# Attention tiles of 64 queries for two heads at once, with a block-diagonal q, in place of tiles of 128 queries of one head

## The chip, the cores and the metric

The kernel runs on one core of a Trainium2 chip. Times are device microseconds from runs on the chip; the lower, the better. The engines are TensorE (PE; PEld is its loading of weights), VectorE (DVE), ScalarE (ACT), GpSimd (POOL) and SyncE (SP), whose queue issues the transfers here.

## The reference

Block-causal attention over 8 batches, 8 heads, 576 positions and a head dimension of 64, followed by a feed-forward layer with a rational activation. A query sees all keys of its own block of 64 and of the blocks before it.

```python
scores = scale * np.matmul(q, k.transpose(0, 1, 3, 2))          # (8, 8, 576, 576), scale = 1/8
mask = (pos[:, None] // 64) >= (pos[None, :] // 64)
scores = np.where(mask, scores, -1000000000.0)
attn = np.exp(scores - np.max(scores, axis=-1, keepdims=True))
attn = attn / (np.sum(attn, axis=-1, keepdims=True) + 1e-09)
x = np.matmul(attn, v)                                          # heads side by side: (4608, 512)
h = x @ w_in                                                    # w_in (512, 2048)
g = (a0 + a1*h + a2*h**2 + a3*h**3) / (1 + |b0|*|h| + |b1|*h**2 + 1e-6)
out = g @ w_out                                                 # w_out (2048, 512)
```

## The kernel before

All values are kept as a high and a low part, both float32r (names that end in h and l), and a product of two such values is made of three matmuls: high by high, high by low, low by high.

Attention walks over 32 pairs of heads (8 batches, 4 pairs each). For a pair, `load` fetches q, k and v, `prep` turns q and k with PE and splits them into `hl`, and six transfers on SP's queue copy the parts into `kq`, one for each head: in it the 64 rows of the head hold qh, kh and kl, and the other 64 rows ql, kh and kl, so that a contraction over 128 rows makes two products in one matmul. `scores` then makes, for each of five tiles of queries (64, 128, 128, 128, 128) and each head, two matmuls (L432, L433) into a bank of PSUM. Widths under 256 are padded to 256. A tile of 128 queries spans two blocks, and a 64-column matmul with `mrow` and `mcol` (L436) puts -2^30 on the last 64 keys for its first 64 queries. DVE takes the negated maximum (L437), `expo` runs the exponential on ACT with its sum (L449), POOL multiplies by the reciprocal of the sum `rc` (L458, L462), and `transp` turns P by PE (L481); ACT copies the turned blocks as the high part and DVE subtracts for the low part (L486, L487) into `pt0`, `pt1`, `pt2`. `pv` multiplies by v (L500). There `vpad` holds v's parts with zeros beside them, so that two heads fall on two halves of the output rows:

```python
for i, (vv, pp) in enumerate(((vh, lo), (vh, hi), (vl, hi))):
    nc.tensor.matmul(o[:, s0:w], lhsT=vblock(vv, x), rhs=pp, ...)
```

over 5 key blocks of 320 or 256 columns and 9 of 256. The result is split again (L503 on ACT, L504 on DVE) and stored to `xscr` in DRAM.

A step is one tile of one head; there are ten to a pair. `attn_steps` gives each part its step: expo one step behind the scores, the transposes 9 behind, pv one more, the load of the next pair at step 0, its prep at 3 and 5. Into these steps two other works are dealt by tables: the splitting of the feed-forward weights into two parts (`split_weights`, most of it in the first 60 steps, the rest up to about step 230), and units of the first half of the feed-forward layer (`Ffn`), which begin when the first batch of x is stored. Feed-forward units are `first` (L207, 256 columns), an activation on ACT, DVE and POOL, and `second` (L257, 512 columns). After the attention the second half of the feed-forward layer follows, with 512 columns in both. The written order is then reordered within each engine by a scheduler that estimates times, so the order on the engines is not quite the written one.

Of the kernel before, what the change touches and what calls it, by code (L numbers as in the profile page):

```python
# [9 lines left out]
F32 = mybir.dt.float32  # L10
F32R = mybir.dt.float32r
# [11 lines left out]
CT = 256  # L23
# [10 lines left out]
OFFS = {5:(0,3,5)}  # L34
G1 = 0
# [26 lines left out]
def attn_ffn_kernel(  # L62
# [241 lines left out]
    NQ = [64, 128, 128, 128, 128]  # L304
    Q0 = [0, 64, 192, 320, 448]
    NK = [64, 192, 320, 448, 576]

    wpool = ctx.enter_context(tc.tile_pool(name="wA", bufs=1))
    with ExitStack() as actx:
# [4 lines left out]

        pt0 = [apers.tile([128, 1, 320], F32R, name=f"pt0{x}") for x in "hl"]
        pt1 = [apers.tile([128, 4, 256], F32R, name=f"pt1{x}") for x in "hl"]
        pt2 = [apers.tile([128, 9, 256], F32R, name=f"pt2{x}") for x in "hl"]

        vpad = [apers.tile([128, 128 + 4 * 192], F32R, name=f"vp{x}") for x in "hl"]
        for x in pt1:  # L320
            nc.vector.memset(x[:, 2:4, 0:128].bitcast(F32), 0.0)
        for x in pt2:
            nc.vector.memset(x[:, 7:9, 0:128].bitcast(F32), 0.0)
        for x in vpad:
            nc.vector.memset(x.bitcast(F32), 0.0)


        NP = B * NPAIR
        if G1:
            visits = ([(p, (0, 1, 2)) for p in range(NPAIR - 1)] + [(NPAIR - 1, (0, 1, 2, 3, 4))]  # L330
                      + [(p, (3, 4)) for p in range(NPAIR - 1)]
                      + [(p, (0, 1, 2, 3, 4)) for p in range(NPAIR, NP)])
        else:
            visits = [(p, (0, 1, 2, 3, 4)) for p in range(NP)]
        NV = len(visits)
        st_ = {}

        def load(p):
            b, hp = divmod(visits[p][0], NPAIR)
            h0 = 2 * hp  # L340

            qr, kr = ((ffn.tile([LP, NL, 2, D], F32, name=f"{n}r{p}", tag="x", bufs=XB) if p < RL else
                       att.tile([LP, NL, 2, D], F32, name=f"{n}r{p}", tag="raw", bufs=1)) for n in "qk")
            vr = att.tile([128, 9, D], F32, name=f"vr{p}", tag="vr", bufs=1)
            for j in range(2):
                nc.sync.dma_start(out=qr[:, :, j, :], in_=q[b, h0 + j].rearrange("(c p) d -> p c d", p=LP))
            for j in range(2):
                nc.sync.dma_start(out=kr[:, :, j, :], in_=k[b, h0 + j].rearrange("(c p) d -> p c d", p=LP))
            for j in range(2):
                nc.sync.dma_start(out=vr[j * 64:(j + 1) * 64, 0, :], in_=v[b, h0 + j, 0:64, :])  # L350
                nc.sync.dma_start(out=vr[:, 1 + j::2, :],
                                  in_=v[b, h0 + j, 64:S, :].rearrange("(c p) d -> p c d", p=128))
            st_[p] = dict(qr=qr, kr=kr, vr=vr)

        def prep(p, which):

            s = st_[p]
            if which == 0:
                s["hl"] = att.tile([128, 4, S], F32R, name=f"hl{p}", tag="hl", bufs=1)
            raw, sc = (s["qr"], s["kr"])[which], (QSCALE, 1.0)[which]  # L360
            hl = s["hl"]
            h, l = (hl[:, 0], hl[:, 3]) if which == 0 else (hl[:, 1], hl[:, 2])
            for half in range(2):
                ps = bank(p - 1, f"tp{p}_{which}_{half}")[:, :3 * LP].rearrange("p (c t) -> p c t", c=3)
                for c in range(3):
                    nc.tensor.transpose(ps[:, c, :], raw[:, half * 3 + c].rearrange("p j d -> p (j d)"),  # L366
                                        ident[:LP, :LP])
                cs = slice(half * 288, half * 288 + 288)
                pf = ps.rearrange("p c t -> p (c t)")
                nc.scalar.activation(out=h[:, cs], in_=pf, func=AF.Copy, scale=sc)  # L370
                nc.vector.scalar_tensor_tensor(out=l[:, cs], in0=pf, scalar=sc, in1=h[:, cs].bitcast(F32),
                                               op0=ALU.mult, op1=ALU.subtract)
            if which == 1:


                for j in range(2):
                    kq = att.tile([128, 3, S], F32R, name=f"kq{p}_{j}", tag="kq", bufs=KQB)
                    src = hl[64 * j:64 * j + 64].bitcast(F32)
                    other = kq[64 - 64 * j:128 - 64 * j].bitcast(F32)
                    nc.sync.dma_start(out=kq[64 * j:64 * j + 64].bitcast(F32), in_=src[:, 0:3])  # L380
                    nc.sync.dma_start(out=other[:, 1:3], in_=src[:, 1:3])
                    nc.sync.dma_start(out=other[:, 0], in_=src[:, 3])
                    s["kq", j] = kq

        def vprep(p):
            vr = st_[p]["vr"]
            at = [lambda x: x[0:64, 0:64].unsqueeze(1), lambda x: x[64:128, 64:128].unsqueeze(1),
                  lambda x: x[:, 128:].rearrange("p (b c) -> p b c", c=192)[:, :, 0:64],
                  lambda x: x[:, 128:].rearrange("p (b c) -> p b c", c=192)[:, :, 128:192]]
            of = [vr[0:64, 0:1], vr[64:128, 0:1], vr[:, 1:9:2], vr[:, 2:9:2]]  # L390
            for f, src in zip(at, of):
                vh, vl = (f(x) for x in vpad)
# [3 lines left out]
        def vblock(x, b):  # L396
            c = 0 if b == 0 else 128 + 192 * ((b - 1) // 2) + 64 * ((b - 1) % 2)
            return x[:, c:c + 128]
# [12 lines left out]
        def pieces(t):  # L411
            return [(0, NK[t])] if t < 4 else [(0, 288), (288, 288)]

        def scores(p, t, j):
            s = st_[p]
            nq = NQ[t]
            if j == 0:
                pt = att.tile([128, 2, NK[t]], F32, name=f"p{p}_{t}", tag=f"p{t}", bufs=1)

                pk = att.tile([128, 2, 64], F32, name=f"pk{p}_{t}", tag="pk", bufs=2) if t > 0 else pt  # L420
                nm = att.tile([128, 2, 2], F32, name=f"nm{p}_{t}", tag="nm", bufs=4)
                sm = att.tile([128, 2, 2], F32, name=f"sm{p}_{t}", tag="sm", bufs=4)
                s[t] = (pt, pk, nm, sm)
            pt, pk, nm, sm = s[t]
            kq = s["kq", j]
            qs = slice(Q0[t], Q0[t] + 128)
            banks = []
            for i, (c0, w) in enumerate(pieces(t)):
                ww = max(w, 256)
                ps = ps_a.tile([128, 512], F32, name=f"s{p}_{t}_{j}_{i}", tag="a")  # L430
                last = t > 0 and c0 + w == NK[t]
                nc.tensor.matmul(ps[:, :ww], lhsT=kq[:, 0, qs], rhs=kq[:, 1, c0:c0 + ww], start=True, stop=False)  # L432
                nc.tensor.matmul(ps[:, :ww], lhsT=kq[:, 0, qs], rhs=kq[:, 2, c0:c0 + ww],  # L433
                                 start=False, stop=not last)
                if last:
                    nc.tensor.matmul(ps[:, w - 64:w], lhsT=mrow, rhs=mcol, start=False, stop=True)  # L436
                nc.vector.reduce_max(out=nm[:nq, j, i:i + 1], in_=ps[:nq, :w], axis=AX.X, negate=True)  # L437
                banks.append(ps)
            if t == 4:
                nc.vector.tensor_tensor(out=nm[:, j, 0:1], in0=nm[:, j, 0:1], in1=nm[:, j, 1:2], op=ALU.min)  # L440
            s[t, j] = banks

        def expo(p, t, j):
            s = st_[p]
            nq, n = NQ[t], NK[t]
            pt, pk, nm, sm = s[t]
            banks = s.pop((t, j))
            for i, (c0, w) in enumerate(pieces(t)):
                nc.scalar.activation(out=pt[:nq, j, c0:c0 + w], in_=banks[i][:nq, :w], func=AF.Exp,  # L449
                                     bias=nm[:nq, j, 0:1], scale=1.0, accum_out=sm[:nq, j, i:i + 1])  # L450
# [3 lines left out]
            if t == 4:  # L454
                nc.gpsimd.tensor_tensor(out=sm[:, :, 0], in0=sm[:, :, 0], in1=sm[:, :, 1], op=ALU.add)
# [176 lines left out]
```

## Time and profile before

| | |
|---|---|
| median of 3 runs | 1382.59 us (1381.54 to 1383.46) |
| span of the profiled execution | 1379.1 us; the page gives no other time of its own for it |
| first and last P times V matmul starting a pair | 41.3 and 968.6 us |
| attention's last matmul | starts at 979.5 us |
| mean granted TensorE clock | 0.974 of full speed, 0.86 in the first 100 us and 0.88 in the second |
| moved by DMA | 200.84 MB, 53.6% of 16 engines' span |

The profile's stretches give, for each, how long every engine was busy, the share of the clock that TensorE was granted, the share of time that the 16 DMA engines were busy, and GB/s. In a group of instructions stand the line, the engine, the operation, what it writes and reads, the shapes and how often; then the time in which the group was busy, the mean duration of one in ns, and the idle time before it with what ended it. A timeline row is start, duration, engine, line. Matmuls overlap, so the distance of two starts says what one costs, not its duration.

### The profile page before, as it was taken

To read this page: it belongs to the slowest core of one execution; us is meant where nothing else is said; L and a number is where in the kernel's file an instruction comes from. 1 tells how busy PE (TensorE), PEld (TensorE's weight loads), DVE (VectorE), ACT (ScalarE), POOL (GpSimd) and SP (SyncE) were. 2 spreads that over 40 slices of the span, in tenths; PEclk is the share of its full clock that TensorE was granted. 3 is DMA by queue.
4 is the path that set the end of the run, shared out by engine and by line. 5 is a ranking of instruction groups with operands and counts; after the bars stand their busy time and mean duration, and the time that the engine had idled before them with its cause. 6 is when DMAs were issued, how large, how long until landed. Compare 5 with 4: busy or idle time off the path is not lost.

```text
span 1379.1 us, 24416 instructions
## 1 busy us (share of the span) xinstructions
PE 1278.1 (93%) x8088; PEld 1149.6 (83%) x8088; DVE 1027.2 (74%) x2048; ACT 909.4 (66%) x2250; POOL 958.2 (69%) x1240
## 2 busy tenths in 40 slices
PE   4677899999899979999999999999989999999997
PEld 3667788999888879888998999998979888888885
DVE  5898877787778857887767777776676767676675
ACT  4766767777677756777767777776645655555553
POOL 4889987687678747777767676666556666666654
PEclk9788999999999999999999999999999999999999
DMA  9778556666556655665654555652632233333332
GB/s 216 198 196 238 146 150 166 168 166 181 148 145 150 164 151 132 165 166 153 157 140 123 154 134 122 160 127 65 213 141 77 77 123 123 122 123 123 122 113 86
DMA packets 216925, 200.84 MB, mean 146 GB/s; under 512 B 129504, under 2 KB 184800, under 8 KB 216800
## 3 DMA queue, kind: packets, MB, share of 16 engines
q1 hardware_dynamic: 216736, 199.28, 53.6%
q8 instruction: 65, 1.06, 0.3%
q14 instruction: 60, 0.49, 0.1%
q0 software_dynamic: 64, 0.00, 0.0%
HBM read 98.57 MB, written 44.04 MB: 103 GB/s over the span
## 4 chain that ended last, share of the span: by engine, by line
PE 69%; DVE 9%; POOL 9%; DMA 5%; ACT 3%; issue 3%; SPq 1%; POOLq 0%; DVEq 0%; ACTq 0%
PE h L207 25%; PE o L257 24%; PE o L500 8%; PE t L481 4%; PE s L432 3%; PE s L433 2%; PE tp L366 2%; POOL gl L240 1%; POOL p L462 1%; DMA x<-xscr 1%; POOL u L217 1%; DVE v L231 1%; DVE nm L437 1%; POOL v L216 1%; DMA xscr<-x 1%
## 5 line engine op out<-in xcount | busy, mean ns | idle before, releaser
L207 PE MATMUL h<-x,wih 128*128 128x256 f32 (+1 forms) x1872 | 415.7, 313 | 9.0 <-DMA x<-xscr 7.9
L207 PEld LDWEIGHTS h<-x,wih 128*128 128x128 f32 x1872 | 309.7, 191 | 29.1 <-issue 6.6
L207 PE MATMUL h<-x,wil 128*128 128x256 f32 (+1 forms) x936 | 290.7, 311 | 0.0
L240 POOL TENSOR_TENSOR gl<-s,gh 128x512 fp32r<-128x512 f32 x144 | 188.8, 1313 | 106.4 <-ACT gh L239 103.0
L257 PE MATMUL o<-woh,gl 128*128 128x512 f32 x576 | 232.2, 403 | 12.1 <-POOL gl L240 10.6
L257 PE MATMUL o<-wol,gh 128*128 128x512 f32 x576 | 227.7, 396 | 0.0
L257 PE MATMUL o<-woh,gh 128*128 128x512 f32 x576 | 227.7, 395 | 0.0
L437 DVE TENSOR_REDUCE nm<-s 128x1 f32<-128x288 f32 (+4 forms) x384 | 161.7, 427 | 78.4 <-PE s L436 45.2
L449 ACT ACTIVATE p<-s,nm 128x288 f32<-128x288 f32 (+4 forms) x384 | 184.9, 485 | 48.3 <-DVE nm L437 35.0
L217 POOL TENSOR_TENSOR u<-v,u 128x512 f32<-128x512 f32 x144 | 189.6, 1317 | 9.8
L216 POOL TENSOR_SCALAR v<-u,bab 128x512 f32<-128x512 f32 x144 | 118.9, 826 | 98.1 <-ACT u L214 94.6
L207 PEld LDWEIGHTS h<-x,wil 128*128 128x128 f32 x936 | 178.7, 191 | 8.7
L462 POOL TENSOR_SCALAR p<-p,rc 128x128 f32<-128x128 f32 (+3 forms) x256 | 164.8, 655 | 29.6 <-DVE rc L457 27.7
L218 DVE TENSOR_TENSOR s<-s,h 128x512 f32<-128x512 f32 x144 | 98.5, 684 | 100.1 <-ACT s L215 99.4
L432 PE MATMUL s<-kq 128*128 128x256 f32 (+3 forms) x384 | 137.3, 360 | 24.3 <-DMA kq<-hl 8.9
L224 ACT ACTIVATE v<-u,qcb 128x512 f32<-128x512 f32 x144 | 104.6, 726 | 69.6 <-POOL u L217 68.9
L214 ACT ACTIVATE u<-h 128x512 f32<-128x512 f32 x144 | 85.9, 596 | 94.2 <-PE h L207 90.1
L239 ACT CAST gh<-s 128x512 fp32r<-128x512 f32 x144 | 89.2, 623 | 82.1 <-DVE s L232 81.5
L257 PEld LDWEIGHTS o<-woh,gl 128*128 128x128 f32 x576 | 109.2, 190 | 35.5 <-POOL gl L240 14.3
L257 PEld LDWEIGHTS o<-wol,gh 128*128 128x128 f32 x576 | 109.1, 189 | 22.2
L257 PEld LDWEIGHTS o<-woh,gh 128*128 128x128 f32 x576 | 109.3, 190 | 18.9
L433 PE MATMUL s<-kq 128*128 128x256 f32 (+3 forms) x384 | 120.1, 315 | 0.0
(105 smaller groups left out, 3043.5 us busy)
## 6 DMA issues: line engine op xcount, KB each, us to landing
kq<-hl SPq DMA_DIRECT2D x64, 432.0 KB, 4.3
kq<-hl SPq DMA_DIRECT2D x64, 288.0 KB, 5.3
x<-xscr SPq DMA_DIRECT2D x56, 256.0 KB, 4.2
xscr<-x SPq DMA_DIRECT2D x32, 320.0 KB, 4.7
qr<-in_q_dram SPq DMA_DIRECT2D x64, 144.0 KB, 2.9
kr<-in_k_dram SPq DMA_DIRECT2D x64, 144.0 KB, 3.0
kq<-hl SPq DMA_DIRECT2D x64, 144.0 KB, 4.8
pscr<-os SPq DMA_DIRECT2D x18, 512.0 KB, 2.9
```

Source lines behind the costliest of these rows:

```text
L207: nc.tensor.matmul(h[:, j, :], lhsT=w[:, dc, fs], rhs=xs[dc][:, hl, :], start=(dc == 0 and i == 0), stop=(dc == 3 and i == 2))
L216: nc.gpsimd.tensor_scalar(out=vt, in0=ut, scalar1=b1, scalar2=b0, op0=ALU.mult, op1=ALU.add)
L217: nc.gpsimd.tensor_tensor(out=ut, in0=vt, in1=ut, op=ALU.mult)
L224: nc.scalar.activation(out=vt, in_=ut, func=AF.Ln, bias=qcb)
L240: nc.gpsimd.tensor_tensor(out=gl.rearrange("p j t -> p (j t)"), in0=st, in1=gh.rearrange("p j t -> p (j t)").bitcast(F32), op=ALU.subtract)
L257: nc.tensor.matmul(self.o[m], lhsT=g[:, j, ms], rhs=w[:, f, :], start=(u == 0 and j == 0 and i == 0), stop=(u == nu - 1 and j == NBU[ph] - ...
L432: nc.tensor.matmul(ps[:, :ww], lhsT=kq[:, 0, qs], rhs=kq[:, 1, c0:c0 + ww], start=True, stop=False)
L433: nc.tensor.matmul(ps[:, :ww], lhsT=kq[:, 0, qs], rhs=kq[:, 2, c0:c0 + ww], start=False, stop=not last)
L437: nc.vector.reduce_max(out=nm[:nq, j, i:i + 1], in_=ps[:nq, :w], axis=AX.X, negate=True)
L449: nc.scalar.activation(out=pt[:nq, j, c0:c0 + w], in_=banks[i][:nq, :w], func=AF.Exp, bias=nm[:nq, j, 0:1], scale=1.0, accum_out=sm[:nq, j ...
L462: nc.gpsimd.tensor_scalar(out=pt[:nq, jj, 64:n], in0=pt[:nq, jj, 64:n], scalar1=rc[:nq, jj:jj + 1], scalar2=1.0, op0=ALU.mult, op1=ALU.mult)
L500: nc.tensor.matmul(o[:, s0:w], lhsT=vblock(vv, x), rhs=pp, start=(x == 0 and i == 0), stop=(x == nb - 1 and i == 2))
```

## The change

Attention is built of tiles of 64 queries of both heads: rows 0 to 63 are the queries of one head, rows 64 to 127 those of the other. For that, `qbd` holds q block-diagonally (128 rows of two heads' dimensions, 128 columns, zeros off the diagonal), two of them for alternate pairs, and k stands as it comes from the transposes, both heads above one another. A tile of block i needs exactly 64(i + 1) keys, so there is no mask, no padding, and no copy into `kq`. The scores take three matmuls. The nine tiles are taken as a whole tile (8) in two pieces of 288 keys, and then in couples of 512 + 64, 448 + 128, 384 + 192 and 320 + 256 keys.

P is turned into 26 slots `ptr`, key blocks of 128, sorted so that the slots of one key block and all its queries lie side by side. P times V is made for each head by two passes, P high and P low, against `vst`, which has v's high and low part side by side, 128 columns: half of the output rows is v high, half v low. Widths are 512, 448, 320, 192 and 64, and four matmuls of 64 for block 0. The two halves must then be added: ACT copies the output as the high part, DVE subtracts its own half for the low part, a transfer `xt` brings the other half across the partitions, and POOL adds it (line 494 of the changed kernel). The lag of the transposes is 8 steps instead of 9, of the two halves of pv 9 and 10. Loads come in other pieces (512 rows by 128 partitions and a tail of 64), with two buffers for q and k instead of one. The feed-forward code stays.

```diff
-    NQ = [64, 128, 128, 128, 128]
-    Q0 = [0, 64, 192, 320, 448]
-    NK = [64, 192, 320, 448, 576]
+    DUOS = [((8, 0, 288), (8, 288, 288))] + [((8 - d, 0, 64 * (9 - d)), (d - 1, 0, 64 * d)) for d in range(1, 5)]
+    def slot(i, kb):
+        return (i, 7 + i, 14 + i, 17 + i, 16)[kb]
...
+        ptr = [apers.tile([128, 26, 128], F32R, name=f"ptr{x}") for x in "hl"]
+        qbd = [[apers.tile([128, 9, 128], F32R, name=f"qbd{i}{x}") for x in "hl"] for i in range(2)]
+        pts = [apers.tile([128, 128 * (i // 2 + 1)], F32, name=f"p{i}") for i in range(9)]
+        vst = apers.tile([128, 5, 2, 128], F32R, name="vst")
...
         def prep(p, which):
-                for j in range(2):
-                    kq = att.tile([128, 3, S], F32R, name=f"kq{p}_{j}", tag="kq", bufs=KQB)
-                    nc.sync.dma_start(out=kq[64 * j:64 * j + 64].bitcast(F32), in_=src[:, 0:3])
-                    nc.sync.dma_start(out=other[:, 1:3], in_=src[:, 1:3])
-                    nc.sync.dma_start(out=other[:, 0], in_=src[:, 3])
+            for c in range(4):
+                nc.tensor.transpose(ps[:, 128 * c:128 * c + 128], raw[:, c].rearrange("p j d -> p (j d)"), ident)
+            if which == 0:
+                for j in range(2):
+                    js = slice(64 * j, 64 * j + 64)
+                    put(qh[js, 0:8, js], ql[js, 0:8, js], ps[js].rearrange("p (c t) -> p c t", c=8), QSCALE)
+            else:
+                put(kh[:, 0:512], kl[:, 0:512], ps, 1.0)
+...
         def scores(p, d, j):
-                nc.tensor.matmul(ps[:, :ww], lhsT=kq[:, 0, qs], rhs=kq[:, 1, c0:c0 + ww], start=True, stop=False)
-                nc.tensor.matmul(ps[:, :ww], lhsT=kq[:, 0, qs], rhs=kq[:, 2, c0:c0 + ww], ...)
-                if last:
-                    nc.tensor.matmul(ps[:, w - 64:w], lhsT=mrow, rhs=mcol, start=False, stop=True)
+            for n, (x, y) in enumerate(((qh, kh), (qh, kl), (ql, kh))):
+                nc.tensor.matmul(ps[:, :w], lhsT=x[:, i, :], rhs=y[:, c0:c0 + w], start=(n == 0), stop=(n == 2))
...
         def expo(p, d, j):
+            for j2 in range(n):
+                x = pts[i][:, 0:64 * (i + 1)]
+                nc.gpsimd.tensor_scalar(out=x, in0=x, scalar1=rc[:, j2:j2 + 1], scalar2=1.0, ...)
...
         def pv(p, j):
+            for kb in range(5):
+                i0 = max(1, 2 * kb)
+                s0 = slot(i0, kb)
+                for n, pp in enumerate(ptr):
+                    nc.tensor.matmul(o[:, 64 * (i0 - 1):512], lhsT=vst[:, kb, j, :], rhs=pp[:, s0:s0 + 9 - i0, js], ...)
+            nc.scalar.copy(out=xh[:, j, 64:S], in_=o)
+            nc.vector.tensor_tensor(out=xl[js, 0, 64:S], in0=o[js], in1=xh[js, j, 64:S].bitcast(F32), op=ALU.subtract)
+            nc.sync.dma_start(out=xt[js, 0], in_=xh[os, j].bitcast(F32))
+            nc.sync.dma_start(out=xscr[b][js, hp, 0, :], in_=xh[js, j].bitcast(F32))
+            if j == 1:
+                nc.gpsimd.tensor_tensor(out=xl.bitcast(F32R), in0=xl, in1=xt, op=ALU.add)
+                nc.sync.dma_start(out=xscr[b][:, hp, 1, :], in_=xl[:, 0])
```

How this stands on the engines, at three places in the middle of the program. PE, the first scores of a pair before (s is the bank of scores, p and pk the multiplied P, h and x the feed-forward unit):

```order
L436 MATMUL s_4_1_1_8433<-mcol,mrow 128x64
L481 MATMUL t_0_0_8477<-ident,p_0_8043 128x64
L432 MATMUL s_0_0_0_8504<-kq_0_8228 128x256
L433 MATMUL s_0_0_0_8504<-kq_0_8228 128x256
L207 MATMUL h_8_1_9046<-x_8_1_8738,wih_142 128x256 x2
L207 MATMUL h_8_1_9046<-x_8_1_8738,wil_143 128x256
```

and PE, scores and transposes after:

```order
L420 MATMUL s_0_1_8488<-k_8153,qbd1h 128x288 x2
L420 MATMUL s_0_1_8488<-k_8153,qbd1l 128x288
L420 MATMUL s_1_0_8541<-k_8153,qbd1h 128x512 x2
L420 MATMUL s_1_0_8541<-k_8153,qbd1l 128x512
L198 MATMUL h_9_0_8809<-x_9_0_8637,wih_148 128x256 x2
```

The scores' operands come straight from the eviction of the transposes, three matmuls to a bank, and the row with the mask is gone.

PE, P times V before: the first key block of a pair, with what is around it.

```order
L481 MATMUL t_2_1_8618<-ident,p_2_8170 128x128 x4
L432 MATMUL s_2_0_0_8636<-kq_0_8228 128x320
L433 MATMUL s_2_0_0_8636<-kq_0_8228 128x320
L436 MATMUL s_2_0_0_8636<-mcol,mrow 128x64
L500 MATMUL o_0_8660<-pt0l,vph 128x320
L500 MATMUL o_0_8660<-pt0h,vph 128x320
L500 MATMUL o_0_8660<-pt0h,vpl 128x320
L366 MATMUL tp_1_0_8680<-ident,kr_8491 128x96 x3
```

and after: the first head's five key blocks.

```order
L487 MATMUL o_0_8739<-ptrl,vst 128x512
L487 MATMUL o_0_8739<-ptrh,vst 128x448
L487 MATMUL o_0_8739<-ptrl,vst 128x448
L487 MATMUL o_0_8739<-ptrh,vst 128x320
L487 MATMUL o_0_8739<-ptrl,vst 128x320
L487 MATMUL o_0_8739<-ptrh,vst 128x192
L487 MATMUL o_0_8739<-ptrl,vst 128x192
L487 MATMUL o_0_8739<-ptrh,vst 128x64
L487 MATMUL o_0_8739<-ptrl,vst 128x64
```

Two passes stand where three were, of falling width; the first matmul, with ptrh and 512 columns, stands six rows further up.

POOL, at the end of a pair before (vpl is v's low part, p_4 the last tile's P):

```order
L462 TENSOR_SCALAR p_3_7388<-p_3_7388,rc_3_7477 128x384 x2
L394 TENSOR_TENSOR vpl<-vr_6665,vph 64x64 x2
L394 TENSOR_TENSOR vpl<-vr_6665,vph 128x4x64 x2
L455 TENSOR_TENSOR sm_4_7486<-sm_4_7486 128x2
L456 TENSOR_SCALAR rc_4_7572<-sm_4_7486 128x2
```

and after:

```order
L397 TENSOR_TENSOR vst<-vr_6392,vst 128x4x128
L397 TENSOR_TENSOR vst<-vr_6392,vst 64x128
L494 TENSOR_TENSOR xl_7102<-xl_7102,xt_7103 128x576
L442 TENSOR_SCALAR rc_4_7223<-sm_4_7134 128x2
L447 TENSOR_SCALAR p_132<-p_132,rc_4_7223 128x320
L447 TENSOR_SCALAR p_131<-p_131,rc_4_7223 128x256
```

The add of the output's halves, which reads the transfer xt, has come in ahead of the last couple's reciprocal and multiplies.

More of the change, by code (lines that the diff above doesn't have):

```diff
@@ L328, in attn_ffn_kernel @@
+        nc.vector.memset(vst[64:128, 4].bitcast(F32), 0.0)
         NP = B * NPAIR
[L329 to L335, printed above, removed]
+        NV = NP
         st_ = {}
         def load(p):
[L339 removed]
+            b, hp = divmod(p, NPAIR)
@@ L349, in load @@
[L349 to L353, printed above, removed]
+            qr, kr = ((ffn.tile([128, 4, 2, D], F32, name=f"{n}r{p}", tag="x", bufs=XB) if p < RL else
+                       att.tile([128, 4, 2, D], F32, name=f"{n}r{p}", tag="raw", bufs=2)) for n in "qk")
@@ L358, in prep @@
             if which == 0:
[L359 to L372, printed above, removed]
@@ L409, in bank, with scores @@
             return pool.tile([128, 512], F32, name=name, tag=tag)
-        def pieces(t):
-            return [(0, NK[t])] if t < 4 else [(0, 288), (288, 288)]
-        def scores(p, t, j):
+        def scores(p, d, j):
             s = st_[p]
-            nq = NQ[t]
             if j == 0:
[L418 to L434, printed above, removed]
-                if last:
[L436 to L441, printed above, removed]
@@ L443, in expo @@
-        def expo(p, t, j):
-            s = st_[p]
[L445 to L450, printed above, removed]
+                s[d] = tuple(att.tile([128, 2], F32, name=f"{n}{p}_{d}", tag=n, bufs=4) for n in ("nm", "sm"))
@@ new lines, in scores, with expo @@
+            if d == 0 and j == 1:
+                nc.vector.tensor_tensor(out=nm[:, 0:1], in0=nm[:, 0:1], in1=nm[:, 1:2], op=ALU.min)
+            s[d, j] = ps
+        def expo(p, d, j):
+            s = st_[p]
+            nm, sm = s[d]
+            if d == 0 and j == 0:
+                return
+            for j2 in (0, 1) if d == 0 else (j,):
+                i, c0, w = DUOS[d][j2]
+                n = 0 if d == 0 else j2
+                nc.scalar.activation(out=pts[i][:, c0:c0 + w], in_=s.pop((d, j2))[:, :w], func=AF.Exp,
+                                     bias=nm[:, n:n + 1], scale=1.0, accum_out=sm[:, j2:j2 + 1])
@@ L507, in attn_ffn_kernel @@
-        items = [(i, t, j) for i, (_, ts) in enumerate(visits) for t in ts for j in range(2)]
-        nxt = [next((n - k for n in range(k + 1, len(items)) if items[n][1:] == items[k][1:]), 99)
-               for k in range(len(items))]
+            rc = att.tile([128, 2], F32, name=f"rc{p}_{d}", tag="rc", bufs=4)
+            n = 2 if d else 1
+            if d == 0:
+                nc.gpsimd.tensor_tensor(out=sm[:, 0:1], in0=sm[:, 0:1], in1=sm[:, 1:2], op=ALU.add)
+            nc.gpsimd.tensor_scalar_add(rc[:, :n], sm[:, :n], 1e-9)
@@ L513, in attn_steps @@
+        items = [(p, d, j) for p in range(NP) for d in range(5) for j in range(2)]
         def attn_steps():
```

213 lines of the change are left out of this document (110 added, 103 removed).

## The prediction

> **What bounds the kernel now.** I read the page first: the busy shares and the chain that ended last.
>
> ```profile
> span 1379.1 us, 24416 instructions
> PE 1278.1 (93%) x8088; PEld 1149.6 (83%) x8088; DVE 1027.2 (74%) x2048; ACT 909.4 (66%) x2250; POOL 958.2 (69%) x1240
> PE 69%; DVE 9%; POOL 9%; DMA 5%; ACT 3%; issue 3%; SPq 1%; POOLq 0%; DVEq 0%; ACTq 0%
> ```
>
> PE carries 69% of the chain. The page says that a busy PE is not PE at its peak, so I then read the stretches, and the lines of the P times V matmuls for where attention lies in the span.
>
> ```profile
> core 0: us, PE busy (x) PEld busy (x) DVE busy (x) ACT busy (x) POOL busy (x), PEclk, DMA share, GB/s
> 50.00:100.00 50.00, 36.82 (x217) 33.11 (x218) 42.58 (x102) 36.40 (x113) 43.17 (x58) 0.83 0.80 208
> 100.00:150.00 50.00, 38.16 (x233) 34.78 (x232) 44.03 (x98) 33.07 (x98) 45.91 (x60) 0.80 0.81 218
> 200.00:400.00 200.00, 187.71 (x1344) 173.53 (x1343) 156.80 (x346) 142.38 (x394) 148.47 (x212) 1.00 0.63 162
> 400.00:600.00 200.00, 188.34 (x1321) 173.94 (x1320) 154.56 (x328) 138.33 (x380) 142.17 (x208) 0.98 0.61 152
> 600.00:800.00 200.00, 194.01 (x1400) 180.65 (x1400) 150.90 (x336) 146.63 (x398) 145.84 (x215) 1.00 0.59 148
> 800.00:1000.00 200.00, 197.53 (x1430) 184.81 (x1428) 144.38 (x303) 142.38 (x364) 134.44 (x195) 1.00 0.51 138
> ...
> L500 PE MATMUL o<-pt0l,vph x32: 306/308/636, 41.3 to 968.6; 128*128 128x320 f32 x32
> ```
>
> There are three stages. Until about 200 us attention runs with the splitting of weights; PE is only 74 to 76% busy in the two rows at the top, DVE and POOL 85 to 92%, and DMA 0.8. From 200 to about 985 us attention and the first feed-forward half share PE, which is busy 767.6 of 800 us (96%), while DVE has 606.6 (76%). Behind that stands feed-forward work that the change does not touch. The 32 head pairs follow each other every (968.6 - 41.3)/31 = 29.9 us, so some 6 lie in the first stage and 26 in the second, where PE's time is what the span is made of.
>
> **What one matmul costs.** Durations in the trace overlap, so I take the distance of starts. For 512 columns, six steps of a steady stream:
>
> ```profile
> 1110.31 0.39 PE L257 MATMUL o<-woh,gl 128*128 128x512 f32 x1
> ...
> 1111.67 0.39 PE L257 MATMUL o<-woh,gl 128*128 128x512 f32 x1
> ```
>
> 1.36/6 = 0.227 us. For narrow ones, two places of the scores with the first DVE reader:
>
> ```profile
> 600.64 0.28 PE L433 MATMUL s<-kq 128*128 128x256 f32 x1
> ...
> 600.96 0.22 DVE L437 TENSOR_REDUCE nm<-s 64x1 f32<-64x64 f32 x1 [0.18 <-PE s L433]
> ```
>
> ```profile
> 608.18 0.28 PE L432 MATMUL s<-kq 128*128 128x256 f32 x1
> 608.30 0.28 PE L433 MATMUL s<-kq 128*128 128x256 f32 x1
> 608.31 0.19 PEld L436 LDWEIGHTS s<-mcol,mrow 128*128 128x128 f32 x1
> 608.42 0.19 PE L436 MATMUL s<-mcol,mrow 128*128 128x64 f32 x1
> 608.43 0.30 PEld L207 LDWEIGHTS h<-x,wih 128*128 128x128 f32 x2
> 608.45 0.49 PE L207 MATMUL h<-x,wih 128*128 128x256 f32 x2
> 608.65 0.36 DVE L437 TENSOR_REDUCE nm<-s 128x1 f32<-128x192 f32 x1 [0.70 <-PE s L436]
> 608.78 0.28 PE L207 MATMUL h<-x,wil 128*128 128x256 f32 x1
> 608.89 0.27 PE L481 MATMUL t<-ident,pk 128*128 128x128 f32 x1
> ```
>
> A 256-column matmul takes 0.119 us. A line between the two gives 0.418 ns a column: 288 cost 132 ns, 320 146, 384 172, 448 199. The 64-column mask is followed 0.03 us later by a pair that takes 0.33 instead of 0.24, so it holds PE for 0.12 us, about a 256-column one. Why decides the change, which makes many matmuls of 64, 128 and 192 columns. Either narrow float32r columns are slow (four times, as 64 against 256 would have it), or each matmul waits for its own weights. The reader tells: DVE starts 0.32 us after the start of the 256-column one and 0.23 after that of the 64-column one. Its columns stream at full rate, 0.09 us sooner; what follows it waits for a weight load that began at 608.43. So up to about 230 columns I charge a floor of 110 ns.
>
> The Trainium skill, "TensorE: Matmul & The Clock Gate", section "Back-to-back issue gap", gives an isolated gap of N/2.4 + 2.5 ns, 29 ns for 64 columns, 82 for 192. By that the sum below would gain another 0.59 us a pair, some 15 us in all. The 0.12 us held by the mask speaks against it, and the same page's section "LDWEIGHTS", P/1.2 (107 ns at 128 columns), agrees with the trace.
>
> **Part 1, PE, per pair.** Scores before: 8 of 256 columns, 4 of 320, 4 of 448, 8 of 288 and 8 masks: 952 + 584 + 796 + 1056 + 880 = 4268 ns. After: three products over widths 288 twice, 512 + 64, 448 + 128, 384 + 192, 320 + 256: 3 x 1456 = 4368. P times V before: 39 of 256 and 3 of 320, 5079 ns; after, two heads by two passes of 512, 448, 320, 192, 64 (791 ns) and four of 64: 3604. The transposes of P stay 25 at 110; those of q and k go from 12 of 96 columns to 9 of 128, which I count even (0.99 us at the floor, against at most 1.32). Sum: +100 - 1475 = -1.38 us a pair, 36 us over 26 pairs and 8 over the first 6.
>
> **Part 2, the other engines, per pair.** Sizes not in the trace are interpolated on these rows.
>
> ```profile
> L437 DVE TENSOR_REDUCE nm<-s 128x1 f32<-128x448 f32 x64 | 39.1, 616 | 5.1 <-PE s L436 4.7
> L437 DVE TENSOR_REDUCE nm<-s 128x1 f32<-128x192 f32 x64 | 22.4, 351 | 12.7 <-PE s L436 12.4
> L371 DVE SCALAR_TENSOR_TENSOR hl<-tp,hl 128x288 fp32r<-128x288 f32 x128 | 55.8, 450 | 16.4 <-ACT hl L370 12.7 <-DMA qr<-in_q_dram 3.2
> L449 ACT ACTIVATE p<-s,nm 128x448 f32<-128x448 f32 x64 | 41.2, 645 | 12.0 <-DVE nm L437 12.0
> L449 ACT ACTIVATION_READ_ACCUMULATOR p<-s,nm 128x1 f32 x320 | 65.5, 205 | 0.0
> L486 ACT CAST pt2h<-t 128x512 fp32r<-128x512 f32 x32 | 18.8, 587 | 5.3 <-PE t L481 5.1
> L486 ACT CAST pt0h<-t 128x128 fp32r<-128x128 f32 x64 | 17.0, 266 | 8.0 <-PE t L481 7.8
> L462 POOL TENSOR_SCALAR p<-p,rc 128x512 f32<-128x512 f32 x64 | 49.6, 785 | 4.3 <-DVE rc L457 4.1
> L462 POOL TENSOR_SCALAR p<-p,rc 128x128 f32<-128x128 f32 x64 | 30.4, 485 | 8.1 <-DVE rc L457 8.1
> L240 POOL TENSOR_TENSOR gl<-s,gh 128x512 fp32r<-128x512 f32 x144 | 188.8, 1313 | 106.4 <-ACT gh L239 103.0
> ```
>
> DVE: 152 + 1.035 ns a column. Maxima: 12 over 3200 columns become 10 over 2880, and one of two minima goes: -1.0 us. Low parts of q and k: 4 at 450 become three of 512 columns (two on 64 partitions, for the block diagonal) and three of 64: +0.9. Low part of the output: 576 columns in 2 become 1152 in 4, since each half of the partitions is read by itself: +0.9. Low parts of P: +0.1. Net +0.9 us.
>
> ACT: two exps and their accumulator reads fewer, 320 columns less: -1.2 us; high parts of q and k +0.75, of the output +0.65, v in two copies instead of four -0.4. Net -0.2 us, even.
>
> POOL: 9 multiplies over 2880 columns instead of 13 over 3200: about -2 us; v in two pieces -0.7; the new add of 576 columns, 1313 x 576/512 = +1.5. Net -1.2 us. The add waits for a transfer, a rival below.
>
> **Part 3, DMA.** The copies of the operands into kq go, six issues a pair on SP's queue; two small ones of half the output come.
>
> ```profile
> 9.40 0.48 SPq L380
> ...
> 14.05 7.26 DMA kq<-hl
> 21.44 0.55 PE s L432
> ...
> kq<-hl SPq DMA_DIRECT2D x64, 432.0 KB, 4.3
> kq<-hl SPq DMA_DIRECT2D x64, 144.0 KB, 4.8
> ```
>
> At the start that path costs 12 us, from 9.40 to 21.44; in its place stand two more evictions on each engine, 1 to 2 us. Later the copies lie behind work already queued, and I count their absence at nothing there; if q and k were late instead, scores would be next to wait. Loads of q, k and v have one more issue each; their buffers are now double, so SP waits less.
>
> **The sum, against the profiled span.** Second stage: of the 36 us I take three quarters, 27, because DVE gets 26 x 0.9 = 23 us more: 630 of 764 us, 82%. The ends are 13 (all of DVE's added time falls on PE) and 36; the row 800 to 1000, where PE is busy 99% beside a DVE at 72%, is nearer to the upper one. First stage: -10 at the start, +0.9 x 6 = +5 where DVE is 85 to 88% busy, PE's 8 us not counted: -5, between -18 and +5. Span: 1379.1 - 32 = 1347. The median of the runs, 1382.59, stands 3.5 above the profiled span, so 1350.
>
> **The rivals.** *DVE takes over.* Speaks for it: PE's busy share falls to 94% in the rows where DVE is at 77 to 78%. Against: the stretch of 800 to 1000. All of DVE's time on the path: 1382.6 - 13, and the start even: 1369.
>
> *POOL waits for xt.* The slower one. The add at line 494 stands in POOL's queue ahead of the next multiplies by rc, and its operand xt comes by a transfer whose like (144 KB) landed after 4.8 us. If w us of that reach PE for each pair, the kernel loses where w passes 1.38; at 2.5 it ends near 1382.6 + 26 x 1.1 - 5 = 1406. Against it: POOL is idle 28% of the second stage, over 8 us a pair, and the multiplies run several items ahead of their transposes.
>
> *Narrow columns at a quarter rate.* 192 columns would cost 333 ns, 128 cost 226: seven and three a pair, +1.9 us against -1.38, or 1382.6 + 14 - 5 = 1392. The reader at 608.65 says no.
>
> *Narrow matmuls below the floor*, by the 29 ns above: 15 us less, 1335.
>
> **How the numbers follow.** My forecast, 1350 within 1335 to 1362: 0.62. DVE takes over, 1369: 0.18. POOL waits: 0.07. Quarter rate: 0.04. Below 1335, by the floor or by a first stage that gains all of its 18 us: 0.09. The range 1328 to 1374 leaves out the two slower ones and a little of the last. A difference under 0.2% (2.8 us) can't be told from no change here; the cases give 0.86 faster, 0.04 same, 0.10 slower.
>
> **What would show it.** Right: the pairs' distance near 28.7 us; 64- to 192-column matmuls about 0.11 us apart; first scores near 11 us; PE above 93% and DVE near 82% from 200 us on. Wrong: 192-column matmuls 0.3 us apart; POOL idle before its add on a DMA with PE idle behind POOL; PE under 90% with DVE as releaser.

## The result: 1.0071 of the time before, where a gain was forecast

The changed kernel takes 1391.85 us (median of five runs, 1388.07 to 1397.17) against 1382.59 us for the kernel before in the same comparison: a ratio of 1.0071, interval 1.0049 to 1.0092. The forecast was 1350. The profiled execution has a span of 1390.1 us and a mean granted TensorE clock of 0.948, against 1379.1 and 0.974. First the page after: span, busy times, and the shares of the chain that ended last.

```profile
span 1390.1 us, 22425 instructions
PE 1264.8 (91%) x7352; PEld 1113.6 (80%) x7352; DVE 1083.2 (78%) x2080; ACT 912.9 (66%) x2154; POOL 959.4 (69%) x1080
PE 55%; DVE 17%; POOL 10%; ACT 8%; DMA 5%; issue 4%; SPq 1%; POOLq 0%; DVEq 0%; ACTq 0%
```

The work left PE as planned (736 matmuls fewer), but PE's share of the chain fell from 69% to 55%, and DVE's rose from 9% to 17%. The stretches after, with the same columns as before:

```profile
50.00:100.00 50.00, 38.62 (x183) 32.56 (x181) 49.27 (x110) 36.93 (x105) 45.12 (x51) 0.71 0.55 158
100.00:150.00 50.00, 32.77 (x160) 29.00 (x161) 48.12 (x98) 33.40 (x91) 41.76 (x47) 0.73 0.55 154
200.00:400.00 200.00, 182.17 (x1156) 164.91 (x1157) 163.56 (x338) 138.16 (x359) 141.90 (x175) 0.95 0.40 108
400.00:600.00 200.00, 179.43 (x1119) 159.85 (x1118) 160.86 (x330) 137.93 (x360) 140.76 (x171) 0.94 0.40 112
600.00:800.00 200.00, 190.99 (x1264) 172.81 (x1263) 161.59 (x350) 146.79 (x381) 145.83 (x182) 0.98 0.35 94
800.00:1000.00 200.00, 189.49 (x1251) 172.08 (x1249) 147.87 (x293) 133.18 (x328) 133.04 (x159) 0.98 0.41 124
```

From 200 to 600 us PE is busy 90 to 91%, and its granted clock is 0.94 to 0.95 where it was 0.98 to 1.00. DVE, at 80 to 82% there, has room; in the first stage it has none (96 to 99%).

Attention runs mixed with feed-forward units, and a faster attention simply leaves more of them for later. A pair distance alone therefore misleads: it is 30.12 us before and 30.10 after. I divide the time up to the last matmul into three parts and take from each the feed-forward matmuls done in it (0.119 us for 256 columns, 0.227 for 512, some 796 us in every kernel). What is left is the time that a part takes beside them. "Start" ends with the P times V of the sixth pair, "second stage" with that of the last pair, and "rest" with the last matmul; all numbers are worked out from starts in the trace, in us, one profiled execution each.

| kernel | start | second stage | rest | sum |
|---|---|---|---|---|
| before | 173.5 | 389.2 | 10.7 | 573.4 |
| changed | 170.3 | 395.9 | 17.6 | 583.8 |
| forecast for the changed kernel | 168.5 | 362 | 10.7 | 541 |

The start came out nearly as forecast. The second stage was to lose 27 us and gained 7, and the rest is 7 longer. Experiments had to tell four theories for the second stage apart, numbered as in the expectations: DVE is the bound (1); POOL's add waits for `xt` (2); the written order and its lag cost the gain (3); or TensorE waits for a bank of PSUM, the memory that matmuls write (4). Attention's scores, transposes and outputs share five such banks, called the ring here; a bank is free again only when its last reader has finished. This is how a wait for a bank looks, in the timeline after (start, duration, engine, line):

```profile
416.16 0.75 ACT L459 CAST ptrh<-t 128x384 fp32r<-128x384 f32 x2
416.67 0.56 DVE L460 TENSOR_TENSOR ptrl<-t,ptrh 128x384 fp32r<-128x384 f32 x1 [1.06 <-ACT ptrh L459]
417.28 1.45 PE L456 MATMUL t<-ident,p 128*128 128x128 f32 x5 [2.76 <-DVE ptrl L460]
```

PE has been idle for 2.76 us when DVE finishes `ptrl`. The transposes that then start read P, which POOL had finished at 398.7, and the identity; nothing that they read comes from that DVE instruction. What ties them to it is the bank `t` that it read: joining writers and readers in the trace, all five banks are in use from 413.66 us until this DVE instruction frees one at 417.22.

### The profile page after: what moved, and what is told of

It is laid out like the page before. It is cut to its first block, busy times and chain, and to the rows that moved or that the text cites. A ratio compares the mean times of both kernels' runs of the same rounds, so it can differ in the third digit from the quotient of the medians.

```text
span 1390.1 us, 22425 instructions
## 1 busy us (share of the span) xinstructions
PE 1264.8 (91%) x7352; PEld 1113.6 (80%) x7352; DVE 1083.2 (78%) x2080; ACT 912.9 (66%) x2154; POOL 959.4 (69%) x1080
## 4 chain that ended last, share of the span: by engine, by line
PE 55%; DVE 17%; POOL 10%; ACT 8%; DMA 5%; issue 4%; SPq 1%; POOLq 0%; DVEq 0%; ACTq 0%
PE h L198 21%; PE o L248 20%; PE o L487 5%; PE s L420 4%; PE t L456 2%; DVE ptrl L460 2%; DVE nm L421 2%; POOL p L447 2%; ACT p L434 2%; POOL u L208 2%; DMA xt<-xh 2%; DVE v L222 1%; DVE u L221 1%; DVE s L223 1%; POOL v L207 1%
## 5 line engine op out<-in xcount | busy, mean ns | idle before, releaser
L198 PE MATMUL h<-x,wih 128*128 128x256 f32 (+1 forms) x1872 | 422.6, 316 | 20.2 <-DMA x<-xscr 10.3
L198 PEld LDWEIGHTS h<-x,wih 128*128 128x128 f32 x1872 | 319.1, 196 | 45.1 <-DMA x<-xscr 11.7
L447 POOL TENSOR_SCALAR p<-p,rc 128x576 f32<-128x576 f32 (+8 forms) x288 | 199.2, 703 | 68.6 <-DVE rc L443 57.5
L434 ACT ACTIVATE p<-s,nm 128x288 f32<-128x288 f32 (+4 forms) x320 | 160.4, 505 | 70.3 <-DVE nm L421 42.3
L198 PEld LDWEIGHTS h<-x,wil 128*128 128x128 f32 x936 | 182.5, 195 | 8.6
L421 DVE TENSOR_REDUCE nm<-s 128x1 f32<-128x288 f32 (+4 forms) x320 | 142.7, 450 | 41.8 <-PE s L420 39.6
L460 DVE TENSOR_TENSOR ptrl<-t,ptrh 128x384 fp32r<-128x384 f32 (+1 forms) x320 | 147.2, 481 | 18.1 <-ACT ptrh L459 16.8
L459 ACT CAST ptrh<-t 128x384 fp32r<-128x384 f32 (+1 forms) x320 | 126.3, 430 | 49.6 <-PE t L456 49.1
L456 PE MATMUL t<-ident,p 128*128 128x128 f32 x800 | 134.5, 291 | 25.0 <-DVE ptrl L460 13.8
L205 ACT ACTIVATE u<-h 128x512 f32<-128x512 f32 x144 | 86.2, 599 | 89.7 <-PE h L198 82.7
L456 PEld LDWEIGHTS t<-ident,p 128*128 128x128 f32 x800 | 100.8, 148 | 43.3 <-issue 7.2
```

The costliest lines, as they stand in the source:

```text
L198: nc.tensor.matmul(h[:, j, :], lhsT=w[:, dc, fs], rhs=xs[dc][:, hl, :], start=(dc == 0 and i == 0), stop=(dc == 3 and i == 2))
L421: nc.vector.reduce_max(out=nm[:, j:j + 1], in_=ps[:, :w], axis=AX.X, negate=True)
L434: nc.scalar.activation(out=pts[i][:, c0:c0 + w], in_=s.pop((d, j2))[:, :w], func=AF.Exp, bias=nm[:, n:n + 1], scale=1.0, accum_out=sm[:, j ...
L447: nc.gpsimd.tensor_scalar(out=x, in0=x, scalar1=rc[:, j2:j2 + 1], scalar2=1.0, op0=ALU.mult, op1=ALU.mult)
L456: nc.tensor.transpose(ps[:, x, :], pts[i][:, 128 * kb:128 * kb + 128], ident)
L459: nc.scalar.copy(out=dh, in_=ps[:, :n])
```

## Experiments

Ratios are to the kernel before, with their intervals; each comparison had its own runs of that kernel, with medians of 1381.42 to 1383.49 us.

### Is it DVE? The maximum over 64 keys, in both kernels

```diff
-            nc.vector.reduce_max(out=nm[:, j:j + 1], in_=ps[:, :w], axis=AX.X, negate=True)
+            nc.vector.reduce_max(out=nm[:, j:j + 1], in_=ps[:, :64], axis=AX.X, negate=True)
```

The edit is shown for the changed kernel; in the kernel before the same line reads `nm[:nq, j, i:i + 1]` and `ps[:nq, :w]`.

> The changed kernel with the maximum taken over the first 64 keys of each piece instead of all of them (the exponential is shifted by another number, the rest is as it was). DVE work falls by 142.7 - 320 x 0.215 = 74 us in all, 2.3 us a pair, twice what the change had added to DVE; nothing else changes. Theory 1 (DVE is what sets the pace of attention after the change): the pairs' distance falls from 29.8 us to about 28.3, the time to 1335 to 1355 us. Theory 2 (the wait of GpSimd's add for the transfer xt) and theory 3 (the written order and its lag, whatever DVE does): within 8 us of 1392.

> Control: the kernel before with the same cut, the maximum over 64 keys only: DVE -79 us. Theory 1, by which the kernel before was bound by TensorE in its second stage (96% busy) and by DVE only in the first 200 us: a gain of 8 to 22 us, 1360 to 1375, clearly less than the changed kernel's gain. If both gain alike, DVE's time was on the path before the change too, and what the change took from TensorE was never worth its count.

The changed kernel: 1376.41 us, ratio 0.9969 (0.9952 to 0.9986). The kernel before: 1370.47, 0.9912 (0.9888 to 0.9936). The two gain in different places:

| kernel | start | second stage | rest |
|---|---|---|---|
| before, 64 keys | 170.4 | 367.6 | 17.3 |
| changed, 64 keys | 163.0 | 397.4 | 11.6 |

The kernel before gains 22 us in its second stage; some of that may be its profiled execution, the fastest of six and 7 us under their median. The changed one gains nothing there, though DVE was relieved as much. The stretches of the changed kernel with 64 keys:

```profile
50.00:100.00 50.00, 37.47 (x197) 31.20 (x196) 46.89 (x110) 38.92 (x113) 43.19 (x50) 0.81 0.59 162
200.00:400.00 200.00, 184.07 (x1121) 163.81 (x1121) 144.39 (x336) 137.87 (x360) 142.41 (x175) 0.91 0.41 112
```

DVE fell from 163.56 to 144.39 of 200 us, and PE, at 184, ran fewer matmuls than with the busier DVE (1121 against 1156) under a lower clock. So the amount of DVE's work does not bound the second stage of the changed kernel; it costs some 7 us at the start. In the kernel before it did cost something in the second stage, though PE was busy 96% there.

### Is it the wait for xt?

The add then reads the low part twice.

```diff
-            nc.sync.dma_start(out=xt[js, 0], in_=xh[os, j].bitcast(F32))
...
-                nc.gpsimd.tensor_tensor(out=xl.bitcast(F32R), in0=xl, in1=xt, op=ALU.add)
+                nc.gpsimd.tensor_tensor(out=xl.bitcast(F32R), in0=xl, in1=xl, op=ALU.add)
```

> The changed kernel without the transfer xt: GpSimd's add reads the low part twice in its place, so the add stays and its wait for the transfer goes (the two halves of the product are not joined in this run). Theory 2 (the wait for xt holds GpSimd's queue and with it the multiplies of P): 15 us or more faster, 1377 or less. Theory 1 (DVE) and theory 3 (order): within 6 us of 1392.

1377.64 us, ratio 0.9968 (0.9957 to 0.998): 14 us less than the changed kernel. The parts are 170.0, 392.4 and 7.2: only 3.5 us come from the second stage and 10 from behind the last pair, where the last feed-forward units wait for the last x (PE stands 5.7 us for that load, 2.1 without `xt`). Not all of the 10 need be the transfer's: with 64 keys, `xt` in place, that wait is 1.4 us. The wait isn't what holds the second stage.

### What do the two passes bring by themselves?

P times V again in three passes, with zeros beside v as in the kernel before, the heads adding into one bank; no halves to join, so `xt` and POOL's add go too.

```diff
+            passes = ((vst[0], ptr[0]), (vst[0], ptr[1]), (vst[1], ptr[0]))
...
-                for n, pp in enumerate(ptr):
-                    nc.tensor.matmul(o[:, 64 * (i0 - 1):512], lhsT=vst[:, kb, j, :], ...)
+                for n, (vv, pp) in enumerate(passes):
+                    nc.tensor.matmul(o[:, 64 * (i0 - 1):512], lhsT=vv[:, kb, 64 * j:64 * j + 128], ...)
```

> The changed kernel with P times V in three passes as before (v's high and low part each with zeros beside it, both heads added into one bank), so the output's halves need not be joined: scores, tiles and transposes as changed. TensorE +1.8 us a pair (36 matmuls for 24, 5.4 us for 3.6), DVE -0.9, ACT -0.6, GpSimd -1.5, the transfer xt gone. If TensorE's matmul time sets the pace: 1392 + 26 x 1.8 = about 1435. Theory 1 (DVE): about 1375, at or below the kernel before. Theory 2: about 1375 too. Theory 3: 1392 to 1410.

1413.94 us, ratio 1.0219 (1.0195 to 1.0242), 22 us slower than the changed kernel; the second stage is 414.2. It lies between the 1435 of PE's time alone and the 1375 of theories 1 and 2. So the two passes with everything they bring along gain 22 us. What loses is, by difference, in the rest of the change: the tiles of both heads, with their loads and their order.

### Is it the banks? Six in the ring, in both kernels

All eight banks were in use: five in the ring, one for `h`, two for the outputs of the two halves of the feed-forward rows. Here both halves add into one bank, so their sums are not kept apart, and the freed one goes to the ring. In the first four pairs the transposes take their banks in turn from the ring, from `h` and from the two outputs; that turn, too, is one bank shorter.

```diff
-                self.o = [(ps_o if m < 2 else ps_b).tile(...) for m in range(nm)]
+                self.o = [(ps_o if m < 1 else ps_b).tile(...) for m in range(nm if ph else 1)]
+                if ph == 0:
+                    self.o = self.o * 2
...
-        ps_a = actx.enter_context(tc.tile_pool(name="ps_a", bufs=5, space=PSUM))
+        ps_a = actx.enter_context(tc.tile_pool(name="ps_a", bufs=6, space=PSUM))
...
-                pool, tag = ((ps_a, "a"), (ps_o, "o0"), (ps_o, "o1"), (ps_h, "a"))[nbank[0] % 4]
+                pool, tag = ((ps_a, "a"), (ps_o, "o0"), (ps_h, "a"))[nbank[0] % 3]
```

> The changed kernel with six PSUM banks for attention instead of five. The sixth is taken from the first feed-forward half: both row halves of a chunk's output add into one bank there (so these sums are not the wanted ones in this run; every matmul, copy and transfer stays). Theory 4 (TensorE waits for banks: in the second stage 89 of 645 bank uses of the changed kernel start within 0.2 us of the release of the bank five uses earlier, 37 of 695 before; a bank is held 3.2 to 4.8 us against 2.5 to 3.1): 15 to 35 us faster than 1392, 1357 to 1377, with the pairs' distance under 29.3 us. Theory 1 (DVE) and theory 3 (order and lag): within 6 us of 1392.

> Control: the same sixth bank given to the kernel before. Theory 4: at most half of what the changed kernel gains, 0 to 10 us, 1372 to 1382, since only 37 of its 695 bank uses start at a release. If it gains as much as the changed kernel, banks bound both alike and do not explain the difference.

The changed kernel: 1352.16 us, ratio 0.9775 (0.975 to 0.9799), 40 us less than with five. The kernel before: 1382.19, 0.9991 (0.9975 to 1.0007), nothing. By parts:

| kernel | start | second stage | rest |
|---|---|---|---|
| before, six banks | 183.8 | 385.8 | 4.4 |
| changed, six banks | 168.3 | 366.2 | 8.1 |

The second stage of the changed kernel falls by 30 us, to 4 above the forecast of 362; that of the kernel before falls by 3. The "nothing" of the kernel before is a sum: its start is 10 longer, its rest 6 shorter. With six banks in both, the change is worth 30 us, 20 of them in the second stage. The page and stretches of the changed kernel:

```profile
span 1348.5 us, 22464 instructions
PE 1250.4 (93%) x7352; PEld 1098.2 (81%) x7352; DVE 1083.3 (80%) x2080; ACT 909.9 (67%) x2154; POOL 955.5 (71%) x1080
...
200.00:400.00 200.00, 189.25 (x1235) 169.92 (x1236) 175.26 (x367) 149.46 (x392) 155.95 (x189) 0.97 0.41 113
400.00:600.00 200.00, 188.34 (x1216) 169.03 (x1214) 169.06 (x354) 145.84 (x386) 150.48 (x186) 0.97 0.43 118
600.00:800.00 200.00, 192.24 (x1292) 175.16 (x1293) 167.84 (x357) 148.40 (x385) 152.57 (x185) 0.99 0.36 97
```

The busy totals of DVE, ACT and POOL are those of five banks within 0.5%, and yet 7 to 9% more matmuls start from 200 to 600 us (1235 against 1156, 1216 against 1119), at a clock of 0.97. DVE stands 88% busy from 200 to 400 us and does not stop it.

The same in four banks:

```diff
-        ps_a = actx.enter_context(tc.tile_pool(name="ps_a", bufs=5, space=PSUM))
+        ps_a = actx.enter_context(tc.tile_pool(name="ps_a", bufs=4, space=PSUM))
```

> The changed kernel with four banks for attention instead of five, nothing left out. Theory 4 (banks): slower by more than the 40 us that the sixth bank gave, 1435 or more. If the sixth bank helped through the feed-forward half that gave it up, and not as a bank of attention: under 1410.

> Control: the kernel before with four banks. Theory 4: it loses too, but less than the changed kernel does, 10 to 40 us (1392 to 1422), since it holds banks for 84 us a pair in sum against 96.

The changed kernel: 1442.31 us, 1.0419 (1.0397 to 1.044). The kernel before: 1454.19, 1.0516 (1.049 to 1.0543), far above what I expected of it. Their second stages are 438.7 and 454.1. With four, five and six banks the kernel before takes 1454, 1383 and 1382 us, the changed one 1442, 1392 and 1352: the first has all that it can use at five, the second not.

### Do the costs add, and does the PE time now count?

Six banks, no `xt` and the maximum over 64 keys together (the three edits above):

> The changed kernel with all three cuts: maximum over 64 keys, no transfer xt, six banks for attention. If the three costs add up: 1392 - 15 - 14 - (what six banks alone give, 15 to 35) = 1328 to 1348, about what was predicted from TensorE's matmul time. If they are one and the same wait seen from three sides: about 1360 to 1370.

1339.4 us, 0.9684 (0.966 to 0.9708): 13 below six banks alone, where the two had brought 14 and 15 at five. They add only in part. Six banks with P times V in three passes (the two edits above):

> Three passes of P times V as in a_pv3, with six banks as in a_ps6 (both row halves of a feed-forward chunk's output add into one bank, so those sums are not the wanted ones in this run). It asks whether TensorE's matmul time counts once banks are there: it has 1.8 us a pair more of it than a_ps6 (1352). If it does in the second stage: 26 x 1.8 = 47 less what its lighter DVE and GpSimd give back, 1380 to 1400. If not: about 1352.

1372.63 us, 0.9921 (0.9898 to 0.9944). The third pass costs 20 us here and 22 at five banks; the sixth bank brings 41 with three passes and 40 with two. So the need for a bank does not come from the joined halves of P times V. By elimination it comes with the rest of the change, of which the tiles of both heads and the way their q and k are turned change what the banks hold; no run takes these two apart.

### A sixth bank without leaving anything out

`h` joins the ring: six banks for both, and feed-forward units take their turn in it.

```diff
-    ps_h = ctx.enter_context(tc.tile_pool(name="ps_h", bufs=1, space=PSUM))
...
-        ps_a = actx.enter_context(tc.tile_pool(name="ps_a", bufs=5, space=PSUM))
+        ps_a = actx.enter_context(tc.tile_pool(name="ps_a", bufs=6, space=PSUM))
...
+        ff.hpools, ff.hbufs = [ps_a], [6]
```

> The changed kernel with nothing left out, and a sixth bank found honestly: the first feed-forward half's tile h takes its banks from attention's ring, now of six, instead of having one to itself. A pair then has 26 uses and some 2.7 of h over six banks, 4.8 a bank, against 5.2 over five. Theory 4 (too few banks): faster than the changed kernel, but by less than with the sixth bank free, 1360 to 1382. If banks are not it: 1392, or slower for h's sharing.

> Control: the same shared ring of six in the kernel before. Theory 4: within 6 us of 1382, as the sixth bank gave nothing there.

Both missed: 1398.89 us, 1.0108 (1.0081 to 1.0134), and 1419.25, 1.0254 (1.0225 to 1.0284). A bank that `h` shares is no sixth bank: in the changed kernel `h` holds one for 7.7 us, 2.6 times a pair, 20 of the 30 us that a bank has. That leaves a third of it; why the kernels then get slower than with five is not shown. With the transposes one step later (`TLAG` 9 instead of 8), expected some us faster, it is slower still:

> The shared ring with the lag of nine steps, which alone took 6 us off the changed kernel. Theory 4 with the lag as a smaller cost of its own: 4 to 8 us under the shared ring alone. A candidate for a version faster than both kernels.

1405.61 us, 1.015 (1.0123 to 1.0178). The lag alone, with five banks:

```diff
-TLAG = 8
+TLAG = 9
```

> The changed kernel with the transposes nine steps behind the scores, as before the change, instead of eight. Theory 3 (the written order and its lag cost the gain): 10 us or more faster, under 1382. The others: within 6 us of 1392.

1385.53 us, 1.0016 (1.0001 to 1.003): 6 us below the changed kernel, with a second stage of 389.7. So the shorter lag was not a gain either, but theory 3 asked for 10 us or more.

Is it the number of uses, or how long one holds? Block 0 of P times V goes into the free quarter of a bank of transposes, one use less in a pair; then also the transposes of q's and k's tails, two less.

```diff
+                if d == 4 and gi == 0:
+                    block0(p, full[:, 384:512])
...
-                ps = bank(p - 1, f"tp{p}_2")
+                ps = spare[p - 2][:, 384:512] if p >= 2 else bank(p - 1, f"tp{p}_2")
```

> The changed kernel with one bank use fewer a pair, nothing left out: the 128 columns of block 0's output stand in the unused quarter of the bank of the last couple's first three transposes. 25 uses instead of 26. If the number of uses is what hurts: 4 to 15 us faster, 1377 to 1388. If it is how long a bank is held (the shared bank is held longer): no gain, 1388 to 1400.

> The same, and the tail transposes of q and k in the unused quarter of another such bank: 24 uses instead of 26. By number: 8 to 30 us faster, 1362 to 1384. By time held: no gain.

1397.55 us, 1.0106 (1.009 to 1.0122), and 1403.68, 1.0145 (1.0128 to 1.0161): slower with each. Fewer uses that hold their bank longer don't help.

## Why the prediction was wrong, step by step

**The price of a matmul was right.** Timeline after, one head's narrow key blocks and the scores behind them:

```profile
624.91 0.25 PE L487 MATMUL o<-ptrh,vst 128*128 128x192 f32 x1
625.00 0.28 PE L487 MATMUL o<-ptrl,vst 128*128 128x192 f32 x1
625.11 0.21 PE L487 MATMUL o<-ptrh,vst 128*128 128x64 f32 x1
625.16 0.28 PE L487 MATMUL o<-ptrl,vst 128*128 128x64 f32 x1
625.27 0.39 PE L420 MATMUL s<-k,qbd0l 128*128 128x320 f32 x1
```

The distances are 90 and 110 ns at 192 columns, 50 and 110 at 64. Over the whole trace the medians are 112 at 64 and 192 columns, 147 at 320, 205 at 448 and 227 at 512. Where the next matmul has the same weights (the ptrh rows here), the medians are 88 at 192 columns and 50 at 64. So the floor holds where new weights follow (not everywhere: 129 of the 800 transposes of P are followed after less than 60 ns, always by a matmul of another line), and the rival of a quarter rate is out. That its price, 1392, is the measured time is a coincidence.

**The copies gone** were right and a little small: the first scores start at 8.8 us, not 11, and the first pair's P times V ends at 43.0 instead of 57.2, 14 us sooner where I counted 10. By the sixth pair 3 of these are left, against 5 forecast.

**DVE** got 56 us more in all, where 0.9 us a pair makes 29. Attention's own lines, summed by group, grew by 32, near the forecast; the rest lies in lines that the change leaves alone, weight splitting and feed-forward above all, and in how far neighbours overlap. POOL, forecast at -1.2 us a pair, stayed even. Groups after (line, engine, shape, count, busy us, mean ns):

```profile
L490 DVE TENSOR_TENSOR xl<-o,xh 64x512 f32<-64x512 f32 x64 | 44.0, 687 | 30.2 <-ACT xh L489 29.4
L423 DVE TENSOR_TENSOR nm<-nm 128x1 f32<-128x1 f32 x32 | 17.4, 543 | 0.0
L447 POOL TENSOR_SCALAR p<-p,rc 128x128 f32<-128x128 f32 x32 | 20.5, 640 | 0.0
L447 POOL TENSOR_SCALAR p<-p,rc 128x64 f32<-128x64 f32 x32 | 16.1, 504 | 0.0
L494 POOL TENSOR_TENSOR xl<-xl,xt 128x576 fp32r<-128x576 f32 x32 | 48.2, 1506 | 21.4 <-DMA xt<-xh 9.4 <-PE h L198 4.5 <-DVE ptrl L460 3.5
```

The output's low part on half the partitions costs what I took, 687 ns for 512 columns. Other sizes were off: a minimum of one column takes 543, and POOL's 128 columns 640 where I had 485. Neither size decided: the rival that DVE takes over fails with the 64-key run, which left the second stage where it was. My sign for it came true in one stretch all the same: PE is 89.7% busy from 400 to 600 us, with DVE's `ptrl` first among the releasers of the transposes. As the example above shows, such a wait can be one for the bank that `ptrl` frees.

**The wait for xt** cost what the last row hints at: POOL stood 9.4 us for the transfer. The run without it gives 14 us in all, and the 3.5 of them in the second stage are 0.13 us a pair, where the rival needed more than 1.38 to make the kernel slower. The transfer itself landed sooner than the 4.8 us that I had from a like one:

```profile
xt<-xh SPq DMA_DIRECT2D x64, 144.0 KB, 2.4
```

**The step that failed** is the sum's second stage: "of the 36 us I take three quarters", with ends 13 and 36. Those ends took for granted that only DVE could stand in the place of PE. PSUM banks were neither a term nor a rival. The pairs' distance was to be 28.7 us; it is 30.10, and 28.46 with six banks, where the second stage comes within 4 us of the forecast. So PE's saving was there to be had, but with five banks it was lost again in PE's waits. The premise that PE's time is what that stage is made of was too strong as well: less DVE work alone shortened it in the kernel before, from 389.2 to 367.6. By joining trace and program order, a bank is held from first write to last read, on the mean of the second stage, for 2.47 us (transposed q, k), 3.06 (scores), 2.55 (P) and 5.77 (output) before, and for 4.80, 3.78, 3.18 and 3.98 after. A pair holds 83.6 us of its 150 bank-microseconds (five banks, 30.1 us) before and 95.9 after. The longest holds after are those of the turned q's bank, 6.8 us, which two copies and two subtractions on 64 partitions read, and of the whole tile's first score bank, 7.4 us (4.5 before), whose exponential waits for a minimum with the second piece. Both changes stand in the diff. But a hold also contains the waits of its readers: with six banks a pair's holds rise to 110 us, so their length alone doesn't show the cause.

The time in which all banks are held says more. The join gives never more than five at once, as it must. From 205 to 905 us all five are held for 13% of the time before and 21% after. Of TensorE's idle stretches over 0.3 us, 15 of 33 us fall into such times before and 45 of 59 after: the whole growth of PE's idle time. With 64 keys it is still 49 of 58 in the changed kernel, and with six banks 32 of 42.

PE's stall then cost twice. Taking each matmul at its slot, PE's time from 200 to 950 us that no matmul fills grew from 43 to 97 us, and time at half clock in the second stage from 7 to 51 us. The second is part of the first: at half clock a 512-column matmul takes 427 ns instead of 227, so 44 us more of it are some 20 of the 54 (an estimate from these two distances). With six banks idle stretches of 1.5 us and more fell from 26 to 7 us (15 before the change), and half clock to 27 us.

The list of releasers shows the wait only weakly, which is a lesson too. Idle before the transposes of P in the whole execution, by what ended it (us, times), before the change:

```profile
  POOL p L462: 5.9, 9
  ACT p L449: 5.1, 9
```

and after:

```profile
  DVE ptrl L460: 19.1, 15
  ACT p L434: 8.7, 7
```

Their releaser changed from their operand to the last reader of a bank. But with six banks the first row still reads 20.5 us, and most of either lies in the start: from 200 to 910 us it is 8.5 with five banks and 7.2 with six. These 19 us aren't the 30 lost; the runs with another number of banks carry the proof, not this list.

**What stays open.** The bank runs show that the changed kernel lacks a bank and the other does not; they don't show which use takes it. Holds fill 64% of the ring after and 56% before, and 65% with six banks, so the average doesn't tell: the waits are local, in the order, and why five suffice at the one and not at the other is not settled; nor why the kernel before loses more at four, nor why the shared ring of six is slower. No version that keeps all of the computation got a true sixth bank. Of the versions that end below both kernels, only the two with the maximum over 64 keys (1370.47 and 1376.41 us) leave nothing out of the sums; they shift the exponential by another number, which is safe only while no score stands far above that maximum.

## What to carry to other kernels

Before crediting saved matmul time, list every ring that matmuls write into: its banks, and for each use the time from the first write to the end of the last reader; a change that adds readers, halves their partitions or lets one bank wait for another may pay there. Count in the trace how long all banks are held at once and how much of PE's idle time falls into it, and run the ring with one bank more and one less, in both kernels, since idle lists don't show it. And where two works share an engine, subtract what was done of the other before comparing a stage.

## What the runs showed of the hardware

The granted clock fell although no idle stretch of PE from 200 to 950 us was over 3.2 us. In these traces it moves in steps of 3.4 us; in the second stage it was halved 11 times after the change, each time behind a step in which matmuls filled 0.46 or less (not behind every such step), and twice before it. The Trainium skill, "TensorE: Matmul & The Clock Gate", section "A second HAM failure mode: psum-queue depth-cycling", tells of a kernel whose short idle times between groups of matmuls, as it goes round PSUM banks, make the clock swing between half and full. The traces of the changed kernel agree: half clock takes 72, 51 and 27 us of the second stage with four, five and six banks. In the kernel before it takes 38, 7 and 17, so the number of banks alone does not set it.
